# Feature map of a linear-attention branch: GpSimd add of two maps, or one VectorE max-add out of PSUM

## The chip, the cores and the metric

The kernel runs on one core of a Trainium2 chip. Its time is the device time of one execution in microseconds (us); before the change the median of three runs is 690.02 us (689.89 to 690.81). A core has five engines with instruction queues of their own: PE (TensorE, with the weight loads shown as PEld), DVE (VectorE), ACT (ScalarE), POOL (GpSimd) and SP (SyncE, which issues most DMAs). Each takes its instructions in the order of the program and waits for the others through semaphores.

## The reference

One input `x` (2048 x 512) goes through two attention blocks with 32 heads of 16, which are mixed by a gate for each row:

```
g = sigmoid((x * gate_w).sum(-1))
a = softmax(q k^T / 4) v @ woA             # q, k, v = x @ wqkvA
phi(t) = where(t > 0, t + 1, exp(t)) + 1e-6
b = (phi(q) kv) / (phi(q) z + 1e-6) @ woB  # kv = sum phi(k) v^T, z = sum phi(k)
out = g * a + (1 - g) * b
```

All inputs are bfloat16. The change concerns `phi`, for the keys and the queries of block B. It can be computed without a branch: phi(t) = max(t, 0) + min(exp(t), 1) + 1e-6.

## The kernel before

**Softmax block.** Its 2048 x 2048 scores for 32 heads are cut into 32 rounds of 64 score blocks, each 128 keys by 512 queries (2048 blocks in all). PE writes a block to one PSUM bank (matmul `ps<-Qz,KT`, made by the helper at L355). Its exponential is taken in one of two ways:

- by ScalarE, two blocks in one instruction (L750, 128 x 1024, into `P`); PSUM banks 0 and 1, or 2 and 3, hold the pair, so ScalarE has two sets;
- by VectorE, one block at a time (L671, from bank 4 or 5 into the int16 tile `Z`, whose bits are then read as bfloat16), with two shifted copies of each pair of blocks, made by VectorE (L728) or GpSimd (L723). Such a block then needs three matmuls with V (`ps<-Z,Vc`), a block of ScalarE one (`ps<-P,Vc`).

The sums with V gather in bank 7 and leave it once in a round (L988 onwards).

**Side tasks.** Projections for both blocks, the gate, and the linear branch run in between as tasks; each takes a PSUM bank, nearly always bank 6, does its matmuls (helper at L361), and gives it back at a FREE step. The linear branch: 16 tasks `t_phik` (L1030) project 128 rows of `x` on the keys' weights and call `phi` (L1019); `t_mt`, `t_z` and `t_kv` make kv and z from them; 16 tasks `t_phiq` (L1075) do the same for the queries; `t_den`, `t_bout` and then `t_final` (with the output projections by `woA` and `woB`) use those. The transposed output of the linear branch and the Q copies of the softmax block go through SP's queue of DMAs.

**`phi` before.** It has two buffers, `eb` and `mb`, of two slots each:

1. L1023, ScalarE: `eb` = exp(bank).
2. L1024, VectorE: `mb` = max(bank, 0) + 1e-6. Then the bank is free.
3. L1026, GpSimd: `eb` = max(min(eb, 1), 0).
4. L1027, GpSimd: destination (bfloat16) = eb + mb. Then the slot is free.

**The order.** No queue is written out by hand. While the program is built, a planner keeps a time for each engine and each resource, offers all steps that could go next as candidates (score groups, V matmuls, L671, L728 or L723, exps, the steps of at most four side tasks, sorted by a deadline given in rounds), takes the one that can start first by its own prices (the number that a step names: 607 ns for `dv(607, ...)`), and appends it to its engine's queue. Who takes the next score block, ScalarE or VectorE, and which engine makes a shift, falls out of this. GpSimd's steps and VectorE's shifts are never planned at the same time (`lock`). Where the planner sees a gap on PE it puts in filler matmuls on the tile `warm`. So an edit in one task changes the order of everything behind it.

Of the kernel before, what the change touches and what calls it, by code (L numbers as in the profile page):

```python
# [8 lines left out]
ALU = mybir.AluOpType  # L9
# [117 lines left out]
def bass_gated_mix__mha_block__linear_attn_block__prompt_kernel(  # L127
# [46 lines left out]
    with ExitStack() as es:  # L174
        _cnt = [0]

        def SB(shape, dt, name):
            _cnt[0] += 1
            return es.enter_context(nc.sbuf_tensor(f"{name}_{_cnt[0]}", list(shape), dt))
# [37 lines left out]
        eb = SB([128, 2, 512], FP32, "eb")  # L217
        mb = SB([128, 2, 512], FP32, "mb")
# [13 lines left out]
        def bank(b, n=1):  # L232
            return ps[:, 512 * b:512 * (b + n)]
# [8 lines left out]
        r_bank = [R(f"bank{b}") for b in range(8)]  # L242
# [18 lines left out]
        r_eb = [R(f"eb{i}") for i in range(2)]  # L261
        r_mb = [R(f"mb{i}") for i in range(2)]
# [589 lines left out]
        def dv(dur, fn, reads, writes):  # L852
            return ("OP", DV, dur, fn, reads, writes, None)

        def ac(dur, fn, reads, writes):
            return ("OP", AC, dur, fn, reads, writes, None)

        def po(dur, fn, reads, writes):
            return ("OP", PO, dur, fn, reads, writes, None)
# [159 lines left out]
        def phi(b, dst_ap, dst_res):  # L1019
            yield ("WAIT", lambda: phi_free[0] or phi_free[1])  # L1020
            i = 0 if phi_free[0] else 1
            phi_free[i] = False
            yield ac(480, lambda: nc.scalar.activation(eb[:, i, :], bank(b), ACT.Exp), [r_bank[b]], [r_eb[i]])  # L1023
            yield dv(607, lambda: nc.vector.tensor_scalar(mb[:, i, :], bank(b), 0.0, 1e-6, op0=ALU.max, op1=ALU.add), [r_bank[b], r_eb[i]], [r_mb[i]])  # L1024
            yield ("FREE", b)
            yield po(640, lambda: nc.gpsimd.tensor_scalar(eb[:, i, :], eb[:, i, :], 1.0, 0.0, op0=ALU.min, op1=ALU.max), [r_eb[i]], [r_eb[i]])  # L1026
            yield po(1300, lambda: nc.gpsimd.tensor_tensor(dst_ap, eb[:, i, :], mb[:, i, :], ALU.add), [r_eb[i], r_mb[i]], dst_res)  # L1027
            phi_free[i] = True

        def t_phik(tb):  # L1030
            b = yield ("BANK",)
            for h in range(2):
                yield pe_step(2, 512, [mmt(bank(b), xT[:, cc, 128 * tb:128 * (tb + 1)], wB[:, cc, D:2 * D], start=(cc == 0), stop=(cc == NCC - 1))
                                       for cc in (2 * h, 2 * h + 1)], [r_xT[tb // 4][h], r_wB], [r_bank[b]])
            yield from phi(b, phiK[:, tb, :], [r_phiK[tb]])
            yield ("FLAG", lambda: flags.add(("phik", tb)))
# [38 lines left out]
        def t_phiq(qc, i):  # L1075
            yield ("WAIT", lambda: "z" in flags and "kv" in flags)
            b = yield ("BANK",)
            for h in range(2):
                yield pe_step(2, 512, [mmt(bank(b), wB[:, cc, 128 * i:128 * (i + 1)], xT[:, cc, 512 * qc:512 * (qc + 1)], start=(cc == 0), stop=(cc == NCC - 1))
                                       for cc in (2 * h, 2 * h + 1)], [r_xT[qc][h], r_wB], [r_bank[b]])  # L1080
            yield from phi(b, phiQT[:, 4 * qc + i, :], [r_phiK[4 * qc + i]])
            yield ("FLAG", lambda: flags.add(("phiq", qc, i)))
# [253 lines left out]
        while True:  # L1336
# [53 lines left out]
            if isinstance(c.fns, tuple) and c.fns[0] == "DMA":  # L1390
                _, o, i, sem, tot, lat, rd, wr, tr, chk = c.fns[1]
# [72 lines left out]
```

## Time and profile before

| what | value |
|---|---|
| median of three runs | 690.02 us (689.89 to 690.81) |
| the profiled execution | 690.02 us |
| its span (first to last instruction) | 688.1 us |
| granted TensorE clock | 1.00 in all stretches but the last (0.99) |
| DMA, HBM read and written | 13 GB/s over the span |
| chain that ended last, by engine | PE 67%, ACT 20%, issue 8% |
| GpSimd idle ahead of L723 | 105.1 us |
| VectorE idle ahead of L671 | 57.8 us |
| ScalarE idle ahead of L750 | 5.6 us |
| first and last start of L1023 | 75.9 and 512.1 us |

How to read it: a row of the groups has the line, the engine, the operation, what it writes and reads, its shape and count, then the busy time in us and the mean ns of one instruction, then the idle time of the engine just before such instructions and what ended most of it. Instructions of one engine overlap at their ends, so the mean length of one can be more than the distance between two starts. `PEld` is the loading of weights. Idle time of an engine that does not bound the kernel costs nothing.

### The profile page before, as it was taken

The numbers are of one execution on the slowest core, as the hardware profiler recorded it, in microseconds if no ns is written. First come the engines' busy times: TensorE is split into PE (matmuls) and PEld (weight loads), VectorE is DVE, ScalarE is ACT, GpSimd is POOL, SyncE is SP. The second block draws the span as 40 slices with busy tenths as digits, with TensorE's granted clock in tenths as the row PEclk, the third lists the DMA queues.
The fourth block names the chain that finished last, engine by engine and source line by source line (L and its number), as shares of the span: only waits on it lengthen the run. The fifth ranks groups of instructions, "written<-read, shape, count | busy, mean of one in ns | idle before, by whom it ended". The sixth has DMA issues, their size and how long they took to land.

```text
span 688.1 us, 24195 instructions
## 1 busy us (share of the span) xinstructions
PE 676.8 (98%) x9923; PEld 204.2 (30%) x9923; DVE 607.2 (88%) x1084; ACT 669.2 (97%) x746; POOL 536.8 (78%) x600
## 2 busy tenths in 40 slices
PE   8899999999999999999999999999999999999998
PEld 3323232222323232222333323232333322222222
DVE  6799989889988898988889888989889899988995
ACT  6899999999999999999999999999999999999995
POOL 3748888887898879886887888878889985588860
PEclk9999999999999999999999999999999999999999
DMA  6920000000000000000000000000011210000001
GB/s 131 301 66 11 6 5 7 2 10 1 5 8 2 9 4 1 10 2 10 2 11 3 4 9 2 10 2 3 17 25 34 49 25 25 17 10 16 18 17 40
DMA packets 27869, 15.97 MB, mean 23 GB/s; under 512 B 19696, under 2 KB 26736, under 8 KB 27760
## 3 DMA queue, kind: packets, MB, share of 16 engines
q1 hardware_dynamic: 26416, 13.91, 7.6%
q8 instruction: 79, 1.29, 0.8%
q10 hardware_dynamic: 1344, 0.52, 0.3%
q14 instruction: 30, 0.25, 0.1%
HBM read 6.69 MB, written 2.10 MB: 13 GB/s over the span
## 4 chain that ended last, share of the span: by engine, by line
PE 67%; ACT 20%; issue 8%; SPq 2%; DVE 1%; DMA 1%; POOL 0%; ACTq 0%; POOLq 0%
PE ps L355 52%; ACT P L750 19%; PE ps L361 15%; SPq L332 2%; ACT eb L1023 1%; DMA xT<-in_A_x_dram 1%; DVE Z L671 0%; POOL Z L723 0%; DVE Zbd L1057 0%; SPq L336 0%; DVE T L988 0%; ACTq L1407 0%; POOL T L1011 0%; ACT wA L1150 0%; POOLq L1407 0%
## 5 line engine op out<-in xcount | busy, mean ns | idle before, releaser
L750 ACT ACTIVATE P<-ps 128x1024 bf16<-128x1024 f32 x707 | 656.8, 1129 | 5.6 <-PE ps L355 5.6
L723 POOL TENSOR_TENSOR Z<-Z,mcon 128x512 int32<-128x512 int32 x408 | 422.9, 1061 | 105.1 <-DVE Z L671 66.1
L671 DVE TENSOR_SCALAR Z<-ps 128x512 int16<-128x512 f32 x634 | 424.6, 682 | 57.8 <-PE ps L355 52.4
L355 PE MATMUL ps<-Qz,KT 32*128 32x512 bf16 x2048 | 276.3, 384 | 2.5 <-ACT P L750 1.2
L355 PE MATMUL ps<-Z,Vc 128*17 128x512 bf16 x1902 | 269.8, 382 | 1.4 <-DVE T L988 1.1
L355 PE MATMUL ps<-P,Vc 128*17 128x512 bf16 x1414 | 246.2, 383 | 0.0
L355 PEld LDWEIGHTS ps<-Qz,KT 32*128 32x128 bf16 x2048 | 68.8, 91 | 263.8 <-ACT P L750 243.7
L728 DVE TENSOR_SCALAR Z<-Z 128x1024 int16<-128x1024 int16 x226 | 92.2, 437 | 0.6
L355 PEld LDWEIGHTS ps<-Z,Vc 128*17 128x17 bf16 x1902 | 61.4, 88 | 71.4 <-issue 42.5
L355 PE MATMUL ps<-warm 128*32 128x512 bf16 (+18 forms) x703 | 76.3, 335 | 1.4 <-POOL warm L408 1.4
L355 PEld LDWEIGHTS ps<-P,Vc 128*17 128x17 bf16 x1414 | 55.8, 88 | 58.3 <-issue 45.8
L1027 POOL TENSOR_TENSOR phiK<-eb,mb 128x512 bf16<-128x512 f32 x32 | 41.0, 1282 | 7.3 <-DVE Z L671 3.0
L361 PE MATMUL ps<-xT,wA 128*32 128x512 bf16 x512 | 43.5, 383 | 0.9 <-DMA xT<-in_A_x_dram 0.6
L355 PEld LDWEIGHTS ps<-warm 128*32 128x32 bf16 (+1 forms) x703 | 23.0, 95 | 20.7 <-issue 14.1
L988 DVE STREAM_TRANSPOSE T<-ps 128x512 f32<-128x512 f32 x32 | 22.8, 712 | 4.7 <-PE ps L355 4.0
L955 POOL TENSOR_SCALAR Vc<-Vc 128x576 bf16<-128x576 bf16 x32 | 21.9, 684 | 5.7 <-DVE Vc L952 2.0
L1026 POOL TENSOR_SCALAR eb<-eb 128x512 f32<-128x512 f32 x32 | 20.0, 625 | 8.0 <-ACT P L750 2.7
L1024 DVE TENSOR_SCALAR mb<-ps 128x512 f32<-128x512 f32 x32 | 21.8, 680 | 2.5 <-ACT eb L1023 1.9
L1011 POOL TENSOR_TENSOR T<-T,rg 128x256 bf16<-128x256 f32 x31 | 19.5, 628 | 5.1 <-DVE Z L728 1.6
L361 PE MATMUL ps<-wA,xT 128*32 128x128 bf16 x1024 | 21.8, 220 | 1.4 <-issue 1.2
L361 PE MATMUL ps<-xT,wB 128*32 128x512 bf16 x256 | 22.9, 383 | 0.0
L1023 ACT ACTIVATE eb<-ps 128x512 f32<-128x512 f32 x32 | 22.8, 714 | 0.0
(80 smaller groups left out, 303.9 us busy)
## 6 DMA issues: line engine op xcount, KB each, us to landing
Qz<-QT SPq DMA_DIRECT2D x120, 16.0 KB, 1.8
wA<-in_A_wqkv_dram SPq DMA_DIRECT2D x1, 1536.0 KB, 7.1
wB<-in_B_wqkv_dram SPq DMA_DIRECT2D x1, 1536.0 KB, 11.7
xnat<-in_A_x_dram SPq DMA_DIRECT2D x3, 512.0 KB, 12.1
out_dram<-outt SPq DMA_DIRECT2D x12, 128.0 KB, 1.7
woA<-in_A_wo_dram SPq DMA_DIRECT2D x1, 512.0 KB, 13.8
woB<-in_B_wo_dram SPq DMA_DIRECT2D x1, 512.0 KB, 9.5
out_dram<-wA SPq DMA_DIRECT2D x4, 128.0 KB, 1.8
```

Source lines behind the costliest of these rows:

```text
L355: return lambda: nc.tensor.matmul(o, lhsT=l, rhs=r, start=start, stop=stop, skip_group_check=sg)
L361: h = nc.tensor.matmul(o[32 * j:32 * j + 32], lhsT=l[:, 32 * j:32 * j + 32], rhs=r, start=start, stop=stop, skip_group_check=True)
L671: return C(DV, 400, 533 * n + 74, lambda: nc.vector.tensor_scalar(o, i, ZB, 0.0, op0=ALU.add, op1=ALU.max), [r_bank[b] for b in bks], r_Z[ ...
L723: return C(PO, 400, 70 + 484 * n, lambda: nc.gpsimd.tensor_tensor(Z[:, z, 0:512 * n].bitcast(I32), Z[:, z0, 0:512 * n].bitcast(I32), mcon[ ...
L728: return C(DV, 450 if hot else 300, 69 + 134 * n, lambda: nc.vector.tensor_scalar(Z[:, z, 0:512 * n], Z[:, z0, 0:512 * n], float(m), None, ...
L750: return C(AC, 500, 427 * n + 49, lambda: nc.scalar.activation(P[:, slot, 0:512 * n], bank(b0, n), ACT.Exp, scale=ESC), [r_bank[b0 + k] fo ...
L955: yield po(690, lambda k=k: nc.gpsimd.tensor_scalar(Vc[:, k, vs].rearrange("p a b c -> p (a b c)"), Vc[:, 0, vs].rearrange("p a b c -> p ( ...
L988: yield dv(607, lambda: nc.vector.transpose(T1[:, a, :], bank(7)), [r_bank[7]], [r_T1[a]])
L1023: yield ac(480, lambda: nc.scalar.activation(eb[:, i, :], bank(b), ACT.Exp), [r_bank[b]], [r_eb[i]])
L1024: yield dv(607, lambda: nc.vector.tensor_scalar(mb[:, i, :], bank(b), 0.0, 1e-6, op0=ALU.max, op1=ALU.add), [r_bank[b], r_eb[i]], [r_mb[i]])
L1026: yield po(640, lambda: nc.gpsimd.tensor_scalar(eb[:, i, :], eb[:, i, :], 1.0, 0.0, op0=ALU.min, op1=ALU.max), [r_eb[i]], [r_eb[i]])
L1027: yield po(1300, lambda: nc.gpsimd.tensor_tensor(dst_ap, eb[:, i, :], mb[:, i, :], ALU.add), [r_eb[i], r_mb[i]], dst_res)
```

## The change

In `phi`, GpSimd's min takes over the constant and comes ahead of VectorE's step; VectorE's step reads the bank and `eb`, adds the two and writes the destination; GpSimd's add and the buffer `mb` are no longer used there. The bank is given back after the new VectorE step, which now waits for GpSimd:

```diff
             yield ac(480, lambda: nc.scalar.activation(eb[:, i, :], bank(b), ACT.Exp), [r_bank[b]], [r_eb[i]])
-            yield dv(607, lambda: nc.vector.tensor_scalar(mb[:, i, :], bank(b), 0.0, 1e-6, op0=ALU.max, op1=ALU.add), [r_bank[b], r_eb[i]], [r_mb[i]])
+            yield po(640, lambda: nc.gpsimd.tensor_scalar(eb[:, i, :], eb[:, i, :], 1.0, 1e-6, op0=ALU.min, op1=ALU.add), [r_eb[i]], [r_eb[i]])
+            yield dv(607, lambda: nc.vector.scalar_tensor_tensor(dst_ap, bank(b), 0.0, eb[:, i, :], op0=ALU.max, op1=ALU.add),
+                     [r_bank[b], r_eb[i]], dst_res)
             yield ("FREE", b)
-            yield po(640, lambda: nc.gpsimd.tensor_scalar(eb[:, i, :], eb[:, i, :], 1.0, 0.0, op0=ALU.min, op1=ALU.max), [r_eb[i]], [r_eb[i]])
-            yield po(1300, lambda: nc.gpsimd.tensor_tensor(dst_ap, eb[:, i, :], mb[:, i, :], ALU.add), [r_eb[i], r_mb[i]], dst_res)
             phi_free[i] = True
```

In the changed kernel the GpSimd min is line 1024 and the VectorE max-add line 1025. The change was named "feature map of the linear branch as one GpSimd min-add and one fused VectorE max-add out of PSUM; first loads over two queues, zeros early"; the diff holds the feature map alone.

## The prediction

> **What bounds the kernel now.** I read the busy shares first, then the windows, then the timeline of ScalarE, the groups and the waits.
>
> ```profile
> span 688.1 us, 24195 instructions
> PE 676.8 (98%) x9923; PEld 204.2 (30%) x9923; DVE 607.2 (88%) x1084; ACT 669.2 (97%) x746; POOL 536.8 (78%) x600
> ```
>
> Two engines, PE and ACT, look full, so shares do not decide. Busy time in stretches of the span (us, then each engine's busy time and instructions) does:
>
> ```profile
> 67.00:250.00 183.00, 182.49 (x2473) 53.73 (x2463) 162.63 (x291) 183.00 (x208) 154.37 (x166) 1.00 0.02 5
> 390.00:520.00 130.00, 127.98 (x1958) 39.09 (x1958) 116.87 (x213) 130.00 (x150) 108.74 (x120) 1.00 0.05 9
> 520.00:655.00 135.00, 134.44 (x1881) 38.48 (x1873) 123.71 (x220) 135.00 (x149) 105.72 (x114) 1.00 0.10 25
> ```
>
> The fourth figure is ScalarE: busy for all of 183, 130 and 135 us. VectorE (third) and GpSimd (last) have some 10 and 15 to 20% left. The feature map runs in the first two of these stretches (its exps start between 75.9 and 512.1 us).
>
> Whether ScalarE is held or truly saturated shows in its timeline (start, length, what):
>
> ```profile
> 72.27 3.84 ACT L750 ACTIVATE P<-ps 128x1024 bf16<-128x1024 f32 x4
> 75.88 0.72 ACT L1023 ACTIVATE eb<-ps 128x512 f32<-128x512 f32 x1
> 76.36 3.91 ACT L750 ACTIVATE P<-ps 128x1024 bf16<-128x1024 f32 x4
> 80.16 0.60 ACT L1023 ACTIVATE eb<-ps 128x512 f32<-128x512 f32 x1
> ...
> 654.71 24.97 ACT L750 ACTIVATE P<-ps 128x1024 bf16<-128x1024 f32 x27
> 683.38 0.59 ACT L1150 CAST wA<-ps 128x512 bf16<-128x512 f32 x1 [3.70 <-PE ps L361]
> ```
>
> Four exps take 75.88 - 72.27 = 3.61 us from start to start, so 0.904 each; a feature map exp takes 76.36 - 75.88 = 0.48. From the first exp (9.68) to the end of the last (654.71 + 24.97 = 679.68) are 670.0 us; 707 x 0.904 + 32 x 0.48 is 654.5. Only some 15 us of 670 are lost, and 5 of those before 50 us, where the order does not change. After 50 us about 0.7 us are lost in each 50, by the distances between starts, in the feature map's stretches no more than elsewhere, and 1.3 us once at 372. So ScalarE's queue is the clock: **time = head (9.7) + exps + tail (8.4, from 679.7 to 688.1)**.
>
> PE's 98% is no bound of its own: the program holds filler matmuls on `warm` that the planner puts into gaps of PE, 44,608 columns singly and 235,264 in fours side by side (58,816 in time); at 512 columns in 0.216 us (below) that is 44 us of PE.
>
> **The change part by part.** Rows used:
>
> ```profile
> L750 ACT ACTIVATE P<-ps 128x1024 bf16<-128x1024 f32 x707 | 656.8, 1129 | 5.6 <-PE ps L355 5.6
> L723 POOL TENSOR_TENSOR Z<-Z,mcon 128x512 int32<-128x512 int32 x408 | 422.9, 1061 | 105.1 <-DVE Z L671 66.1
> L671 DVE TENSOR_SCALAR Z<-ps 128x512 int16<-128x512 f32 x634 | 424.6, 682 | 57.8 <-PE ps L355 52.4
> L728 DVE TENSOR_SCALAR Z<-Z 128x1024 int16<-128x1024 int16 x226 | 92.2, 437 | 0.6
> L1027 POOL TENSOR_TENSOR phiK<-eb,mb 128x512 bf16<-128x512 f32 x32 | 41.0, 1282 | 7.3 <-DVE Z L671 3.0
> L1026 POOL TENSOR_SCALAR eb<-eb 128x512 f32<-128x512 f32 x32 | 20.0, 625 | 8.0 <-ACT P L750 2.7
> L1024 DVE TENSOR_SCALAR mb<-ps 128x512 f32<-128x512 f32 x32 | 21.8, 680 | 2.5 <-ACT eb L1023 1.9
> L1111 DVE TENSOR_TENSOR wA<-ps,wA 128x512 bf16<-128x512 f32 x16 | 10.9, 679 | 1.0 <-DMA xnat<-wA 0.7
> ```
>
> *Removed:* 32 GpSimd adds (L1027): 41.0 us of GpSimd. *Replaced at one price:* the min on GpSimd (0.625 each) keeps its shape and has another second operation. *Changed:* VectorE's max reads PSUM and now also a float32 SBUF operand and writes bf16. The trace has no such instruction; the nearest row (L1111: PSUM and SBUF in, bf16 out) costs 0.679 against 0.680 now. Bounds from VectorE's rows of 128x512 out of PSUM, 0.63 (shortest L1024) to 0.71 (the transposes at L988): -1.6 to +1.0 us of VectorE over 32. I take 0.68, the row with both kinds of operand, so nothing.
>
> *What the freed time turns into.* The planner rebuilds the whole order, and the two programs' orders can be counted. ScalarE: 707 exps of score pairs become 701. VectorE: 634 score blocks (L671) become 646, 226 shifts (L728) become 211. GpSimd: 408 shifts (L723) become 435. PE: 24 more matmuls on V, since a block through VectorE needs three in place of one. Hence:
> - GpSimd: -41.0 + 27 x 1.04 (422.9/408) = -13 us. It can.
> - VectorE: +12 x 0.67 (424.6/634) - 15 x 0.41 (92.2/226) = +1.9 us, against 57.8 us that it idles ahead of L671. It can.
> - PE: +24 matmuls, four side by side in 0.216 us (16 take 684.23 - 683.37 = 0.86), +1.3 us; 4 fewer groups of score matmuls, -0.9; fillers fall by 6,784 columns, at 512 in 0.216, -2.9. It can.
> - ScalarE, the clock: **-6 x 0.904 = -5.4 us**. This holds if its waits stay at what they are.
>
> [...] The trace shows an overlap of 1129 - 904 = 225 ns, and the measured spacing stands.
>
> *The tail.* The key and query feature maps end later in the order: the last query one comes after exp 534 of 701, before after 525 of 707. So more of the output projection is left: behind the last score matmul stand 112 + 16 matmuls of L361, not 112. The tail is bound by PE (from 678.7 to 685.3 it never stops), so **+0.9 us** (16 in 0.86).
>
> *The new wait.* VectorE's max-add waits for GpSimd's min, which waits for the exp and for whatever GpSimd does. From the exp's start: 0.72, then up to one shift in progress (1.06), then 0.61: 1.3 to 2.4 us, where the old max could start at 0.72. Behind it on VectorE stand the score blocks (L671), which free banks 4 and 5 for PE's next score group, which feeds ScalarE. If nothing covered it, 32 x (0.61 to 1.67) = 20 to 53 us of VectorE. Cover: the planner puts each max-add where, by its own prices, the min is done, and lets score blocks and shifts go ahead of it until then; it prices the min at 640 ns (trace 625) and the max-add at 607 (L671's blocks, priced alike, follow each other in some 600); and the score banks of ScalarE are double. The same kind of wait stands now on GpSimd (8.0 and 7.3 us ahead of L1026 and L1027), and costs ScalarE nothing. So 0 taken, 0 to +4 kept. If the cover is gone, each uncovered microsecond is one of the span.
>
> *Held longer, moved.* PSUM bank 6, the one that serves all side tasks, is held until the max-add, some 0.6 to 1.7 us more for each of 32; its effect is the later tail above. `eb` comes free earlier, at the max-add and not after the 1.28 us add. On the SP queue all 16 transposes of the linear branch now stand ahead of the last 16 Q copies; before, 14 did and the other two between. Of these, the first eight start after score group 591 and are needed near 612 (round 28 of 32): 20 groups x 0.93 = 19 us, against 4.94 for eight copies and 1.8 to land. Hidden. Loads at the start: nothing moves, and the words about first loads and zeros name no edit. The order is the same up to the first feature map.
>
> [...]
>
> **Sum**, against the profiled execution: span 688.1 - 5.4 + 0.9 = 683.6; that execution took 690.02, 1.92 around the span, which is also the median of the three (689.89 to 690.81). **Forecast 685.5 us.**
>
> **The rivals.**
> 1. *Waits of ScalarE shrink too*, as GpSimd has more room and VectorE's shifts come earlier: up to 3 more, some 1.3 of it the one loss at 372 us: 682.5 to 683.8. For: L723 idles 105 us for VectorE, not the reverse. Against: losses are evenly small.
> 2. *The new wait eats part*: 2 to 3 us of waits reach ScalarE: 687.5 to 688.6. For: the longer chain in front of VectorE. Against: 0.7 us lost in 50, the feature map's stretches included.
> 3. *PE is the real clock.* Then -2.5 (+1.3 - 0.9 - 2.9) + 0.9: 688.4, and with a few waits no change. For: 98%. Against: the fillers, and ScalarE without a gap.
> 4. *Slower:* VectorE stalls at its queue's head. GpSimd is some 80% busy, so a min meets on average half a shift, 0.5 us; if that shows in each max-add and delays banks 4 and 5, 32 x 0.5 = 16 us of VectorE, of which PE's spare score bank covers half: +8, so 693.5. It decides from 4.5/32 = 0.14 us of ScalarE per feature map on (no gain), and 0.18 for slower by 0.2%. For: one in-order queue carries both. Against: the planned order, and 57.8 us of idle on VectorE.
>
> **How the numbers follow.** Forecast 684.0 to 687.4: 0.68. Rival 1: 0.05. Rival 2: 0.07. Rival 3, within 0.2% (1.4 us, about what a measurement of this kernel can tell from no change): 0.08. Rival 4: 0.12. Faster: 0.68 + 0.05 + 0.07 = 0.80. The range goes from 683.5 (part of rival 1) to 689.0 (rival 2 and the lower edge of rival 3): about 0.8.
>
> **What would show it.** Right: 701 exps at 0.904, ScalarE again full in the middle windows, no GpSimd add, the max-add near 0.68, the tail behind the last exp some 9.3 us. Wrong: ScalarE gaps beside L1025 with "VectorE from GpSimd L1024" among the waits; a max-add over 0.8; ScalarE gaps after 620 us that end at a Q copy. It would be off most if the planner's order held ScalarE idle somewhere that counts cannot show.

## The result and the profile after

The changed kernel takes 713.46 us (median of four runs, 710.67 to 714.96) against 689.95 before (689.87 to 690.81): 1.033 times the time before, interval 1.030 to 1.037. The forecast was 685.5. The profiled execution took 710.67, with a span of 708.8; it had a granted clock of 1.00 and is the fastest of the four, the other three had 0.993 to 0.998.

The head of the changed kernel's page, and the first line of the chain that ended last, by engine, before and after:

```profile
span 708.8 us, 24205 instructions
PE 675.1 (95%) x9945; PEld 203.9 (29%) x9945; DVE 610.5 (86%) x1081; ACT 669.3 (94%) x740; POOL 563.9 (80%) x595
...
PE 67%; ACT 20%; issue 8%; SPq 2%; DVE 1%; DMA 1%; POOL 0%; ACTq 0%; POOLq 0%
...
PE 52%; ACT 17%; POOL 14%; issue 8%; DVE 8%; DMA 1%; ACTq 0%; POOLq 0%; DVEq 0%
```

The first chain line is that of before, the second that of the changed kernel. GpSimd was to lose 13 us and gained 27 (536.8 to 563.9); it has 0% of the chain before and 14% now. ScalarE has six exps fewer and is no longer full. The same stretches as before:

```profile
67.00:250.00 183.00, 171.81 (x2337) 50.06 (x2335) 154.94 (x276) 173.59 (x195) 156.82 (x153) 1.00 0.02 5
390.00:520.00 130.00, 120.71 (x1606) 34.82 (x1607) 112.76 (x204) 122.63 (x139) 98.84 (x95) 1.00 0.02 4
520.00:655.00 135.00, 129.82 (x2159) 40.62 (x2151) 120.99 (x211) 131.72 (x145) 118.15 (x124) 1.00 0.12 27
```

In the fourth figure, the busy time of ScalarE, 9.4, 7.4 and 3.3 us are missing, in the stretches where the feature map runs and behind it. The groups name the culprit:

```profile
L750 ACT ACTIVATE P<-ps 128x1024 bf16<-128x1024 f32 x701 | 654.4, 1090 | 25.6 <-PE ps L355 25.0
L723 POOL TENSOR_TENSOR Z<-Z,mcon 128x512 int32<-128x512 int32 x435 | 448.1, 1056 | 93.7 <-DVE Z L671 74.9
L671 DVE TENSOR_SCALAR Z<-ps 128x512 int16<-128x512 f32 x646 | 430.9, 682 | 50.2 <-PE ps L355 45.4
L728 DVE TENSOR_SCALAR Z<-Z 128x1024 int16<-128x1024 int16 x211 | 89.1, 444 | 0.7
L1024 POOL TENSOR_SCALAR eb<-eb 128x512 f32<-128x512 f32 x32 | 62.4, 1949 | 22.7 <-ACT eb L1023 7.2
L1025 DVE SCALAR_TENSOR_TENSOR phiK<-ps,eb 128x512 bf16<-128x512 f32 x32 | 22.1, 692 | 26.1 <-POOL eb L1024 26.1
L1111 DVE TENSOR_TENSOR wA<-ps,wA 128x512 bf16<-128x512 f32 x16 | 10.8, 676 | 2.1 <-DMA xnat<-wA 1.9
```

L1024, GpSimd's min, now takes 1949 ns where L1026 took 625, on the same 128 x 512 float32 elements; in the instruction itself, only the second operation and its constant differ (add 1e-6 for max 0). The means of the other GpSimd and VectorE rows lie within 2% of before. L1025, the row below, says that VectorE stood idle for it for 26.1 us in all.

One feature map in the timeline, engine by engine (start, length, what; in brackets the idle time before and what ended it):

```profile
82.50 2.13 POOL L1024 TENSOR_SCALAR eb<-eb 128x512 f32<-128x512 f32 x1
...
84.66 0.69 DVE L1025 SCALAR_TENSOR_TENSOR phiK<-ps,eb 128x512 bf16<-128x512 f32 x1 [1.81 <-POOL eb L1024]
...
85.41 0.61 PE L361 MATMUL ps<-wB,xT 128*32 128x512 bf16 x8 [1.40 <-DVE phiK L1025]
...
86.17 0.39 PE L355 MATMUL ps<-Qz,KT 32*128 32x512 bf16 x3
...
86.61 1.94 ACT L750 ACTIVATE P<-ps 128x1024 bf16<-128x1024 f32 x2 [1.43 <-PE ps L355]
```

The long min holds VectorE; the max-add gives PSUM bank 6 back late; the next side task's matmul, which writes that bank, is at the head of PE's queue (L361, waiting 1.40 us for L1025) and holds the score matmuls behind it; ScalarE, for which PE can have two score groups ready at most, runs dry for 1.43 us. Three of these waits over the whole execution (us in total, times, longest):

```profile
DVE phiK L1025 <- POOL eb L1024: 26.1, 32, 1.8
ACT P L750 <- PE ps L355: 25.0, 41, 1.4
PEld ps L361 <- DVE phiK L1025: 19.6, 22, 1.7
```

### The profile page after: what moved, and what is told of

It reads as the page before. It is cut to its first block, busy times and chain, and to the rows that moved or that the text cites. A ratio compares the mean times of both kernels' runs of the same rounds, so it can differ in the third digit from the quotient of the medians.

```text
span 708.8 us, 24205 instructions
## 1 busy us (share of the span) xinstructions
PE 675.1 (95%) x9945; PEld 203.9 (29%) x9945; DVE 610.5 (86%) x1081; ACT 669.3 (94%) x740; POOL 563.9 (80%) x595
## 4 chain that ended last, share of the span: by engine, by line
PE 52%; ACT 17%; POOL 14%; issue 8%; DVE 8%; DMA 1%; ACTq 0%; POOLq 0%; DVEq 0%
PE ps L355 38%; ACT P L750 16%; PE ps L361 14%; POOL eb L1024 8%; POOL Z L723 5%; DVE Z L671 3%; DVE phiK L1025 2%; DVE Z L728 1%; DMA xnat<-wA 1%; ACT eb L1023 0%; DVE Zbd L1057 0%; POOL T L1011 0%; POOL Vc L955 0%; DVE T L988 0%; DVE OAT L1015 0%
## 5 line engine op out<-in xcount | busy, mean ns | idle before, releaser
L750 ACT ACTIVATE P<-ps 128x1024 bf16<-128x1024 f32 x701 | 654.4, 1090 | 25.6 <-PE ps L355 25.0
L723 POOL TENSOR_TENSOR Z<-Z,mcon 128x512 int32<-128x512 int32 x435 | 448.1, 1056 | 93.7 <-DVE Z L671 74.9
L671 DVE TENSOR_SCALAR Z<-ps 128x512 int16<-128x512 f32 x646 | 430.9, 682 | 50.2 <-PE ps L355 45.4
L355 PE MATMUL ps<-Z,Vc 128*17 128x512 bf16 x1938 | 274.9, 382 | 4.1 <-POOL Z L723 2.0
L728 DVE TENSOR_SCALAR Z<-Z 128x1024 int16<-128x1024 int16 x211 | 89.1, 444 | 0.7
L1024 POOL TENSOR_SCALAR eb<-eb 128x512 f32<-128x512 f32 x32 | 62.4, 1949 | 22.7 <-ACT eb L1023 7.2
L355 PE MATMUL ps<-warm 128*32 128x512 bf16 (+14 forms) x701 | 71.2, 335 | 1.4 <-POOL warm L408 1.4
L361 PE MATMUL ps<-xT,wA 128*32 128x512 bf16 x512 | 43.1, 383 | 4.3 <-DVE phiK L1025 4.3
L1025 DVE SCALAR_TENSOR_TENSOR phiK<-ps,eb 128x512 bf16<-128x512 f32 x32 | 22.1, 692 | 26.1 <-POOL eb L1024 26.1
L361 PE MATMUL ps<-xT,wB 128*32 128x512 bf16 x256 | 22.4, 383 | 4.0 <-DVE phiK L1025 4.0
L361 PE MATMUL ps<-wA,xT 128*32 128x128 bf16 x1024 | 21.7, 220 | 4.0 <-DVE phiK L1025 2.5
L361 PE MATMUL ps<-wB,xT 128*32 128x512 bf16 x256 | 22.1, 382 | 1.6 <-DVE phiK L1025 1.6
L361 PE MATMUL ps<-phiK,xnat 128*32 128x512 bf16 x256 | 22.8, 382 | 0.0
L361 PE MATMUL ps<-woA,OAT 128*32 128x512 bf16 x256 | 21.7, 382 | 0.0
## 6 DMA issues: line engine op xcount, KB each, us to landing
wB<-in_B_wqkv_dram SPq DMA_DIRECT2D x1, 1536.0 KB, 11.5
```

The source lines that it names most:

```text
L355: return lambda: nc.tensor.matmul(o, lhsT=l, rhs=r, start=start, stop=stop, skip_group_check=sg)
L361: h = nc.tensor.matmul(o[32 * j:32 * j + 32], lhsT=l[:, 32 * j:32 * j + 32], rhs=r, start=start, stop=stop, skip_group_check=True)
L671: return C(DV, 400, 533 * n + 74, lambda: nc.vector.tensor_scalar(o, i, ZB, 0.0, op0=ALU.add, op1=ALU.max), [r_bank[b] for b in bks], r_Z[ ...
L723: return C(PO, 400, 70 + 484 * n, lambda: nc.gpsimd.tensor_tensor(Z[:, z, 0:512 * n].bitcast(I32), Z[:, z0, 0:512 * n].bitcast(I32), mcon[ ...
L728: return C(DV, 450 if hot else 300, 69 + 134 * n, lambda: nc.vector.tensor_scalar(Z[:, z, 0:512 * n], Z[:, z0, 0:512 * n], float(m), None, ...
L750: return C(AC, 500, 427 * n + 49, lambda: nc.scalar.activation(P[:, slot, 0:512 * n], bank(b0, n), ACT.Exp, scale=ESC), [r_bank[b0 + k] fo ...
```

## The experiments

Theory P: the pair of operations, min-add, sets GpSimd's price, and the longer instruction in an order planned for 0.64 us is the whole loss. Rivals: C, the instruction is slow because of what runs beside it; W, the new wait of VectorE at the head of its queue costs, however short the min is. Times are medians. The kernel before, run beside them on the same chip, took 690.0 us beside e1, e2 and e3, 691.1 beside e4, e5, e6 and e9, and 690.4 beside e1b, e10 and e11; each comparison is with the one beside it. The edits are shortened: `eb` stands for `eb[:, i, :]`, `...` for arguments that stay, and the lists of resources are left out.

### GpSimd alone, pairs of operations (m1_pairs)

```diff
+ for k in range(4): gpsimd.tensor_scalar(dst, src, 1.0, 0.0, op0=min, op1=max)    # float32 128x512; 13 other pairs or constants, two single operations; four in bfloat16
```

> Leaves the whole computation out (the output is zeros): GpSimd alone runs two-operation instructions of 128x512, four of each pair of operations, with no other engine at work. Theory P (the pair of operations sets GpSimd's price): min-add takes 1.9 to 2.0 us in float32 alone too, min-max 0.6. Theory C (contention: the min-add is slow because of what VectorE and ScalarE do beside it in its new place): all pairs take 0.6 us. What the other pairs take is not foreseen by either.

Rows of min-max (L30), min-add (L32), mult-add (L48) and the min alone (L58), with nothing beside them:

```profile
L58 POOL TENSOR_SCALAR dst<-src 128x512 f32<-128x512 f32 x4 | 5.9, 1487 | 0.3
L48 POOL TENSOR_SCALAR dst<-src 128x512 f32<-128x512 f32 x4 | 2.5, 621 | 0.3
...
L32 POOL TENSOR_SCALAR dst<-src 128x512 f32<-128x512 f32 x4 | 7.7, 1920 | 0.3
...
L30 POOL TENSOR_SCALAR dst<-src 128x512 f32<-128x512 f32 x4 | 2.5, 614 | 0.3
```

Min-add takes 1920 ns without any neighbour: theory C is out. (The source tile holds 0.5 everywhere; in the kernel, on real data, the same pair takes 1949.) Of the sixteen, four are short: min-max 614, add-mult 619, mult-mult 620, mult-add 621. Nine pairs take 1916 to 1926: min-add (with 1e-6 and with 1.0), min-min, max-min, max-add, add-min, add-max, add-add, mult-max, min-mult. One operation alone is not the cheapest: min 1487, add 1491. The pairs that were tried in bfloat16 have the same prices there (min-max 614, mult-mult 620, min-add 1922 and 1919).

### The fused max-add with min-max (e1_minmax, again as e1b_minmax)

```diff
- po(640, lambda: nc.gpsimd.tensor_scalar(eb, eb, 1.0, 1e-6, op0=ALU.min, op1=ALU.add))
- dv(607, lambda: nc.vector.scalar_tensor_tensor(dst_ap, bank(b), 0.0, eb, op0=ALU.max, op1=ALU.add))
+ po(640, lambda: nc.gpsimd.tensor_scalar(eb, eb, 1.0, 0.0, op0=ALU.min, op1=ALU.max))
+ dv(607, lambda: nc.vector.scalar_tensor_tensor(dst_ap, bank(b), 1e-6, eb, op0=ALU.max, op1=ALU.add))
```

> The changed kernel with the pair min-max on GpSimd as before, and the constant 1e-6 as the lower bound of VectorE's max (which differs from adding it by 1e-6 at most). The order of all instructions is that of the changed kernel. Theory P: L1024 takes 0.62 us, VectorE waits under 8 us for it in all in place of 26.1, ScalarE's idle time ahead of L750 falls from 25.6 to about 6, and the time is what was forecast for the change, 685.5 (684 to 688). Theory C: L1024 stays near 1.95 us and the time near 711. Theory W (a wait of VectorE on GpSimd at its queue's head is what costs, whatever the min's length): L1024 0.62, but VectorE waits 10 us or more, and the time is 692 to 700.

> The same kernel as the first with min-max and the fused max-add, beside the two others on one chip: 0.998 of the time before, 686.5 to 689.5.

Measured: 688.32 us, 0.998 of before (0.9964 to 0.9992); again 688.50, 0.997 (0.995 to 0.9992). Each instruction stands where it stands in the changed kernel; groups of the first:

```profile
L750 ACT ACTIVATE P<-ps 128x1024 bf16<-128x1024 f32 x701 | 651.8, 1135 | 8.1 <-PE ps L355 8.0
...
L1025 DVE SCALAR_TENSOR_TENSOR phiK<-ps,eb 128x512 bf16<-128x512 f32 x32 | 21.6, 675 | 0.0
L1024 POOL TENSOR_SCALAR eb<-eb 128x512 f32<-128x512 f32 x32 | 20.2, 632 | 25.6 <-ACT eb L1023 7.9
```

The min is back at 632 ns, VectorE does not wait for it at all (0.0), and the loss of 23.5 us is gone. Theory W is out: the new wait is there in the order and costs nothing while the min has the length that the planner believes. What is left is the change as it was meant, worth -1.7 to -1.9 us, not the -4.5 of the forecast; 688.32 lies just above the 684 to 688 that theory P gave.

### The kernel before with min-add (e2_before_minadd)

```diff
- po(640, lambda: nc.gpsimd.tensor_scalar(eb, eb, 1.0, 0.0, op0=ALU.min, op1=ALU.max))
+ po(640, lambda: nc.gpsimd.tensor_scalar(eb, eb, 1.0, 1e-6, op0=ALU.min, op1=ALU.add))    # and VectorE's step adds 0.0, not 1e-6
```

> The kernel before, in its order, with the pair min-add on GpSimd (1e-6 moved there from VectorE's step): no new wait for VectorE, no fused max-add. Theory P: L1026 takes 1.95 us, GpSimd has 42 us more to do, some of its shifts come late, and the time rises to some 695 to 710. Theory C: L1026 0.62 and 690, no change. Theory W: L1026 may be 1.95, but without VectorE waiting for it the time stays within 690 to 693.

Measured: 713.86 us, 1.034 (1.033 to 1.036): a loss as large as that of the changed kernel, without the fused instruction and without VectorE waiting for the min. It is above the 695 to 710 that theory P gave. Two rows and three waits:

```profile
L728 DVE TENSOR_SCALAR Z<-Z 128x1024 int16<-128x1024 int16 x226 | 106.8, 501 | 0.6
L1026 POOL TENSOR_SCALAR eb<-eb 128x512 f32<-128x512 f32 x32 | 62.2, 1943 | 6.9 <-DVE Z L728 2.0
...
PEld ps L355 <- POOL Z L723: 30.4, 51, 1.4
ACT P L750 <- PE ps L355: 19.6, 34, 1.4
...
PE ps L355 <- POOL Z L723: 15.4, 19, 1.2
```

The way to ScalarE is another one here: GpSimd's shifts (L723) come late, PE's V matmuls wait for them, the score matmuls wait behind those (PEld's wait for L723 was 7.6 us in all before, 30.4 here). VectorE's shifts (L728) also take 501 ns in place of 437, 14.6 us more in all; that is a second way in which this order loses, and its share was not separated. So the new wait of the changed kernel is not needed for the loss. An engine that is 78% busy on average is not free: in a planned order it runs late 1.3 us in 32 places, and in-order queues pass that on by whichever semaphore comes first.

### A short pair and one operation (e5_mult_add, e4_min_only)

Both are in the changed kernel's order, with another GpSimd step. Mult-add leaves out the cap of the exponential at 1, so it computes another function and is a probe of time alone.

```diff
+ nc.gpsimd.tensor_scalar(eb, eb, 1.0, 1e-6, op0=ALU.mult, op1=ALU.add)    # e5
+ nc.gpsimd.tensor_scalar(eb, eb, 1.0, None, op0=ALU.min)                  # e4, 1e-6 as in e1
```

> The changed kernel with the pair mult-add in place of min-add on GpSimd (it leaves out the cap of the exponential at 1). Theory P: mult-add is one of the short pairs (0.62 alone), so L1024 takes 0.63 us and the time is that of min-max, 688.3 (687 to 690). If the add or the constant 1e-6 is what costs, or the place of the instruction: 1.95 us and 710 or more.

> The order of the changed kernel, with GpSimd doing the min alone (one operation; the constant as the lower bound of VectorE's max), which took 1.49 us by itself in the run of pairs. Theory P as a dose: of the 25 us between min-max (688.3) and min-add (713.5), the share (1.49 - 0.63)/(1.95 - 0.63) = 0.65 is paid: 705 (700 to 708). A threshold instead (the planned order absorbs up to about one us more): 690 to 695. If one operation is cheaper in place than two: 0.6 and 688.

Mult-add: 689.35 us, 0.997 (0.995 to 0.998), L1024 at 634 ns. Neither an add in second place nor the constant costs by itself; the pair min-add does. The min alone: 697.88 us, 1.012 (1.009 to 1.016); its row:

```profile
L1024 POOL TENSOR_SCALAR eb<-eb 128x512 f32<-128x512 f32 x32 | 49.7, 1553 | 22.0 <-ACT eb L1023 7.3
```

Both guesses missed: it is neither in proportion (705) nor absorbed (690 to 695). Against the kernel before beside them, mult-add, the min alone and min-add (the changed kernel) stand at -1.8, +6.8 and +23.5 us: the first 0.92 us more (634 to 1553 ns) cost 8.6, 0.27 per feature map, the last 0.40 (to 1949) another 16.7, 0.52 each. By the executions with a granted clock of 1.00 (two of the min alone, 696.50 and 696.72; one of min-add, 710.67) the last part costs 14.1, 0.44 each, about its length. So the planned order takes up most of a small delay and little or nothing of what goes beyond; whether the last part costs more than its length is not shown by so few.

### Half of the feature maps (e9_keys_only)

```diff
- yield from phi(b, phiK[:, tb, :], [r_phiK[tb]])
+ yield from phi(b, phiK[:, tb, :], [r_phiK[tb]], True)    # keys: min-add; queries: min-max; else as e1
```

> The order of the changed kernel, min-add on GpSimd for the 16 key feature maps only, min-max for the 16 of the queries. Theory P, each instruction paying for itself: half of the 25 us, so 700 to 702, with ScalarE's waits between 67 and 250 us as in the changed kernel (some 10 us more than before) and few after. If a late start of the linear branch is what costs (a chain that runs on into the queries): over 705. If only the crowded query part costs: 690 or less.

Measured: 700.33 us, 1.014 (1.011 to 1.016). From mult-add (-1.8) to min-add (+23.5) are 25.3 us, and this run, at +9.2, has 11.0 of them: a little under the half that theory P has, and within its 700 to 702. In two stretches (again ScalarE is the fourth figure):

```profile
67.00:250.00 183.00, 170.03 (x2339) 50.25 (x2341) 154.99 (x276) 173.82 (x195) 156.25 (x152) 1.00 0.02 5
390.00:540.00 150.00, 146.82 (x2111) 43.96 (x2105) 139.12 (x252) 150.00 (x173) 107.02 (x122) 1.00 0.02 4
```

ScalarE misses 9.2 us where the keys' maps run, as in the changed kernel (9.4), and none where the queries' run. Each map pays where it stands.

### The right price for the planner (e3_priced, e11_priced_q)

```diff
- yield po(640, lambda: nc.gpsimd.tensor_scalar(eb, eb, 1.0, 1e-6, op0=ALU.min, op1=ALU.add))
+ yield po(2000, lambda: nc.gpsimd.tensor_scalar(eb, eb, 1.0, 1e-6, op0=ALU.min, op1=ALU.add))
- add_task(t_q(n // 4, n % 4), max(0, 2 * n - 4), 2 * n - 1, ...)                      # e11 alone
+ add_task(t_q(n // 4, n % 4), max(0, 2 * n - 4), 2 * n - (4 if n > 11 else 1), ...)
```

> The changed kernel, with the planner told 2000 ns for the min-add in place of 640; the planner rebuilds the order (706 exps, 636 score blocks on VectorE, 409 shifts on GpSimd). Theory P with the wrong price as the way it costs: L1024 1.95 us, VectorE waits under 8 us for it, time 688 to 693. If the length itself costs by holding bank 6 and VectorE's queue, not the order made for another price: VectorE still waits over 15 us, time 697 or more. Theory C: as the changed kernel, 705 or more, with L1024 at a length that varies.

With the price alone: 714.82 us, 1.035 (1.034 to 1.036). Both branches of the expectation fell. VectorE's idle time ahead of L1025 is 0.0, so the wait was planned away, and the time did not move. ScalarE shows where it went (a stretch, then three lines of its timeline):

```profile
520.00:655.00 135.00, 125.91 (x1968) 39.05 (x1965) 109.60 (x194) 119.51 (x132) 90.01 (x94) 0.96 0.13 25
...
565.59 2.85 ACT L750 ACTIVATE P<-ps 128x1024 bf16<-128x1024 f32 x3 [4.78 <-PE ps L355]
...
618.51 1.94 ACT L750 ACTIVATE P<-ps 128x1024 bf16<-128x1024 f32 x2 [7.05 <-PE ps L355]
621.26 1.02 ACT L750 ACTIVATE P<-ps 128x1024 bf16<-128x1024 f32 x1 [0.81 <-PE ps L355]
```

In the stretch ScalarE misses 15.5 of 135 us, where before it is full, and the granted clock is 0.96 (0.988 to 0.990 over each of the four executions). PE's timeline names the releaser of the second gap:

```profile
617.93 0.97 PE L355 MATMUL ps<-Qz,KT 32*128 32x512 bf16 x6 [3.75 <-DMA Qz<-QT]
```

Our reading: feature maps of 2 us hold bank 6 longer and the side tasks run late as a whole (the 16 transposes of the linear branch start on SP's queue at 573.77 us, with min-max at 534.12). The projections of the last queries' Q then come when their round has begun; two of them stand behind all 16 transposes on SP's queue, the order that the prediction called hidden. So the second run brought the last four projections of Q forward:

> Min-add at its full length, priced at 2000 ns, with the last four Q projections brought forward. Theory Q (with the right price the loss moved from VectorE's wait to late Q copies, 18 us of ScalarE between 550 and 625): those waits go, some 8 us more tail since 148 more output projection matmuls stand behind the last score, so 700 to 705 in place of 714.8. If the length of the min-add costs through GpSimd's and bank 6's time in any order: 710 or more.

Measured: 701.91 us, 1.017 (1.016 to 1.018), as theory Q had it. The gaps are gone (idle time ahead of L750 24.0 to 9.4), and the tail behind the last exp is 700.5 - 684.2 = 16.3 us (8.4 before), with 260 matmuls of output projections behind the last score matmul (112 before). With the right price the kernel is still 11.5 us behind the one before, and 7.9 of these are tail.

### More pairs (m2_pairs)

```diff
+ for k in range(4): gpsimd.tensor_scalar(dst, src, 0.3, -0.7, op0=min, op1=max)    # eight other pairs or single operations, three at 128x1024, two tensor_tensor
```

> Leaves the whole computation out (the output is zeros): GpSimd alone, more pairs and 128x1024. If the price goes by the pair alone: min-max 0.61 with other constants too, and at 1024 elements min-max takes some 1.1 us and min-add 3.7 us, a price per element and not a fixed one. If the constants 1.0 and 0.0 are what makes min-max short: 1.9 us with 0.3 and -0.7.

Min-add (L55), mult-add (L57) and min-max (L53) at 128 x 1024, and min-max with 0.3 and -0.7 (L35):

```profile
L55 POOL TENSOR_SCALAR dst<-src 128x1024 f32<-128x1024 f32 x4 | 14.5, 3628 | 0.3
...
L57 POOL TENSOR_SCALAR dst<-src 128x1024 f32<-128x1024 f32 x4 | 4.2, 1048 | 0.3
L53 POOL TENSOR_SCALAR dst<-src 128x1024 f32<-128x1024 f32 x4 | 4.2, 1041 | 0.3
L35 POOL TENSOR_SCALAR dst<-src 128x512 f32<-128x512 f32 x4 | 2.5, 614 | 0.3
```

The other constants leave the price of min-max as it is (614 ns with both), and from 512 to 1024 elements the price rises by (1041 - 614)/512 = 0.83 ns an element for min-max, (3628 - 1920)/512 = 3.34 for min-add, four times as much. Max-max, mult-subtract, subtract-mult, add-subtract, mult-min and max-mult take 1919 to 1926 at 512; mult alone 1492, max alone 1487; adding or multiplying two tensors 1262.

### What is missing to the forecast (e6_spread, e10_spread_q)

With min-max, 2.6 to 2.8 us of the forecast gain are missing. In e1's profile ScalarE is full between 390 and 540 us and has 113.02 of 115 between 540 and 655, where before it has 115:

```profile
540.00:655.00 115.00, 112.42 (x1677) 32.96 (x1681) 102.80 (x178) 113.02 (x124) 98.67 (x105) 1.00 0.14 30
```

There the linear branch's division and output tasks (L1095 to L1111) stand close together behind the last feature map. The loss is not a fixed one: in the same order ScalarE idles 8.1 us ahead of L750 in e1's profile, 7.6 in e1b's and 6.5 in e5's (mult-add), against 5.6 before. The granted clock has a part in the medians too. It was under 1.00 in 11 of the 24 executions with min-max (0.993 to 0.999), which go up to 694.0 us, and in 5 of the 40 of the kernel before beside them. Among those with 1.00 the gain is 2.1 us (687.96 against 690.02) and 3.3 (687.06 against 690.35). Why this order gets the lower clock more often is not known.

Two runs spread the tasks out:

```diff
- add_task(t_den(qc), 15 + 2.4 * (qc + 1), 25, ...)      # and t_bout, the same
+ add_task(t_den(qc), 15 + 2.4 * (qc + 1), 24, ...)      # e6 and e10; e10 also has e11's deadlines of Q
```

> The kernel with min-max and the fused max-add, with the deadlines of the linear branch's division and output tasks at round 24 in place of 25, so that they go in between the query feature maps and are not crowded behind the last one. Theory L (what is missing to the forecast, 2.5 us, is lost where those outputs crowd: VectorE's L1111 waits for the transposes on the SP queue, PE for VectorE, ScalarE for PE, at 536 to 570 us): no wait of L1111 over 1 us in all, ScalarE's idle time ahead of L750 falls from 8.0 to 6, time 685.5 to 687. Rival: the loss is that of a tighter schedule anywhere: 688 to 689.

Measured: 696.23 us, 1.008 (1.006 to 1.011), a miss: one Q copy came late (ScalarE's longest wait is 7.6 us), so it does not decide whether the crowding of those tasks is the loss.

> Min-max and the fused max-add, the division and output tasks at deadline 24 (spread between the query feature maps), and the deadlines of the last four Q projections brought forward to the round of their release, so that the spread does not push a Q copy late as it did in the run before (7.7 us of ScalarE at 558). Theory L: no Q copy late, L1111 waits under 1 us, ScalarE's idle time ahead of L750 about 6, time 686 to 688, a little under the kernel without the spread in the same call. If the order of side tasks is all used up and each move only shifts the loss: 688 to 692.

Measured: 688.61 us, 0.998 (0.997 to 0.999), against 688.50 for the kernel without the spread beside it. No Q copy is late, the row of ScalarE improves a little, L1111 still waits 2.4 us for transposes, and the tail is longer (10.1 us, against 9.1 in e1):

```profile
L750 ACT ACTIVATE P<-ps 128x1024 bf16<-128x1024 f32 x701 | 651.2, 1130 | 6.6 <-PE ps L355 6.6
...
L1111 DVE TENSOR_TENSOR wA<-ps,wA 128x512 bf16<-128x512 f32 x16 | 10.9, 684 | 2.4 <-DMA xnat<-wA 2.4
```

Theory L is not confirmed. That this version beats the kernel before by 0.2 to 0.3% is measured; why it does not by 0.65% stays open, beyond the place of some of the waits and the lower clock.

## Why the prediction was wrong

- **The step that failed** is the one that read "*Replaced at one price:* the min on GpSimd (0.625 each) keeps its shape and has another second operation". A row was used for an operation that it does not hold. Shape, type, engine and instruction were the same, one of two operations was not, and the price went from 0.625 to 1.949 us: 32 x 1.32 = 42 us of GpSimd. GpSimd's sum of -13 us came out at +27, and the fused kernel's gain at a loss of 23.5 us.
- It was not counted as an operation that the trace lacks, though the trace of before has no min-add on GpSimd. Had it been, the nearest rows would have bounded it by 0.61 to 1.28 us (L1026 and L1027, both 128 x 512 from float32 on GpSimd), which still misses 1.95, but would have opened the range upwards.
- **Rival 4 had the sign and part of the way**: VectorE stalls at its queue's head, and the loss reaches ScalarE. Its price (0.5 us on average) was the wait behind a shift in progress; the wait came from the min itself (26.1 us over 32, 0.82 each; with the short min it is 0.0). It was said to go through banks 4 and 5; the feature map shown above loses through bank 6, whose next task stands in PE's queue ahead of the score matmuls. So its sign came true by another cause than the one it gave.
- **Right**, as the run with min-max shows: ScalarE sets the time; 701 exps; the max-add at 0.675 to 0.692 us (0.68 taken); no cost of the new wait when the min is short (0.0 us ahead of L1025); the tail longer by 0.6 us (9.03 in the changed kernel, 699.77 to 708.8, and 9.1 with min-max, against 8.4; 0.9 forecast); nothing at the start (first exp of a score pair at 9.68 us before, at 9.65 in the changed kernel).
- **Mis-sized there**: with min-max, waits of ScalarE were to stay what they are, and grew by 2.5 us in e1 (5.6 to 8.1 ahead of L750), 2.0 of them between 540 and 655 us. That is the size of rival 2, and 688.3 lies in its range, but not by its way: VectorE did not wait for the min at all. The Q copies behind the transposes, called hidden, were hidden in this order, and became the largest loss (7 us in one gap) when the feature maps were planned longer.

## What to carry to other kernels

When one operation of a two-operation instruction changes, its row in the trace is no price for the new pair (here 0.614 us for min-max and 1.920 for min-add); measure the pair alone: four instructions gave 1.920 us here, and 32 in the kernel 1.949. In an order that a planner laid out instruction by instruction, 1.3 us more on an engine with 20% to spare cost more than half of themselves (23.5 of 42 us), by whichever in-order queue meets it first, and giving the planner the right price moved the loss to later tasks, first to late Q copies, then to a longer tail. Test a fused instruction with each of its parts at the old price before judging it: here the fusion gains 0.2 to 0.3%, and its companion, the min-add, alone loses 3.4% (e2).

## What the runs showed of the hardware

GpSimd's `tensor_scalar` on 128 x 512 in float32, alone, took one of three lengths in the two runs (m1, m2): 0.61 to 0.62 us for min-max, mult-add, add-mult and mult-mult, 1.49 for a single operation (min, max, add and mult), and 1.92 to 1.93 for every other pair tried, fifteen of them. In bfloat16 only min-max (614 ns), mult-mult (620) and min-add (1919 and 1922) were tried, with the same prices. A single operation cost more than a short pair: min-max with a lower bound that never binds, at 614 ns, is 2.4 times as fast as min, at 1487. Order can count: min-max took 614 and max-min 1916, while mult-add took 621 and add-mult 619. A kind of operation can count: add-mult took 619 and subtract-mult 1926. Why these four are short was not tried.

VectorE's shift (L728, int16) took 437 ns on average in the kernel before and 501 with min-add in the same order (e2); the second operation of GpSimd's min and the constants are all that differs there. In the changed kernel's order the shift took 444 ns with min-add and 440 with min-max (e1). So the longer shift shows in one order alone, beside a longer min; by which GpSimd instruction it comes, and how, was not tried.

From 512 to 1024 elements mult-add rose from 621 to 1048 ns, (1048 - 621)/512 = 0.83 ns an element as with min-max, against 3.34 for min-add. The other pairs and the single operations were not run at a second size.
